# Fused linear attention and long convolution on one core: two stretches of the hand-written schedule put in a new order, with fourteen steps on other engines

## The chip, the cores and the metric

The kernel runs on one NeuronCore of a Trainium2 chip. The core's engines each work through their own list of instructions in order and meet only through semaphores: TensorE (PE, with its weight loads shown apart as PEld), VectorE (DVE), ScalarE (ACT), GpSimd (POOL), and SyncE (SP), which here only starts DMA transfers. The metric is the device time of one execution in microseconds. Three timed executions of the kernel before took 295.18, 297.97 and 299.99 us (median 297.97). The profile is of one more execution, which took 295.91 us.

## The reference

Eight batches go through two layers. The first is linear attention over 8 heads, 576 positions and 64 channels:

```python
def phi(x):
    proj = np.einsum('bhsd,df->bhsf', x, w_phi)            # 64 -> 128 features
    proj = proj - np.max(np.abs(proj), axis=-1, keepdims=True)
    return np.concatenate([np.exp(proj), np.exp(-proj)], axis=-1)
q_p, k_p = phi(q), phi(k)
kv  = np.einsum('bhsf,bhsd->bhfd', k_p, v)
num = np.einsum('bhsf,bhfd->bhsd', q_p, kv)
den = np.einsum('bhsf,bhf->bhs', q_p, np.sum(k_p, axis=2))[..., None] + 1e-06
x   = num / den                       # heads side by side: [8, 576, 512]
```

The second is a gated convolution along the sequence, done by Fourier transform:

```python
proj = x @ w_proj                     # 512 -> 3 * 512: x1, x2, x3
conv = irfft(rfft(x2, axis=1) * rfft(filter_fft, axis=0), n=576, axis=1)
out  = (x1 * conv * x3) @ w_out       # float32, [8, 576, 512]
```

## The kernel before

**The plan.** No scheduler and no pool decides the order. `PLAN` (lines 30 to 197) is a long string of words, and `run` (lines 1039 to 1043) calls one method for each word from left to right. A word is the name of a step and its arguments, with the first PSUM bank behind an `@`: `X1,3,1@5` is step X1 of batch 3, block 1, written to bank 5; a step that needs two banks takes the next one as well. Where a step can run on either of two engines, the word names the engine (`Fe,ACT,2,1@0`). Since each engine is in order, the order of the words of one engine is the order of its instructions; semaphores follow from what is read and written. Four batches or so are in flight at once, so the words of one batch stand between those of others.

```python
        for word in PLAN.split():
            name, _, bank = word.partition("@")
            self.bank = int(bank) if bank else None
            f, *args = name.split(",")
            getattr(self, f)(*[int(a) if a.isdigit() else a for a in args])
```

**The steps of one batch b**, in the order of the data:

- `load` (POOL queue, L595) brings q, k or v in; `trh` (SP queue, L607) transposes a half of q or k into qT or kT.
- `Pk`, `Pkt` (PE, L635, L650) project k. Out of PSUM, `ex,k,p` and `ex,k,m` (ACT, L697) take the two exponentials, and `maxk` (DVE, L715) the maximum. `Qn`, `Qnt` project q for `maxq` alone. `mhi` (ACT), `mlo` (DVE or POOL, L739), `trm` (PE) and `trme` (a copy) bring the maxima of q into a transposed form mT; `Pq`, `Pqt` (PE, L669, L675) project q again with them subtracted, and `ex,q` (ACT) takes the exponentials.
- `em` (ACT, L751) and `vs` (POOL, L757) scale v; `KV` (PE, L772) is the sum over positions, `KVe` its copy; `NE`, `NEt` (PE, L786, L795) give numerator and denominator; `rc` and `xn` (DVE, L800, L805) divide. `xn` is written into one buffer, a quarter v at a time.
- `trx` (SP queue, L824) transposes a quarter of xn into xT, `trxt` (L829) the rest; for the last quarter of batch 6 `ptx` and `ptxe` do it on PE and DVE. `X1` and `X3` (PE, L916) read all four quarters of xT.
- `f1`, `f2` (POOL or DVE, L853, L859) are sums and differences of xn for the Fourier transform; `Ft`, `Fs` (PE, L868, L875) transform, `Fe` (a copy, ACT L297 or DVE L299) writes XF, `X2` (PE, L894) projects, `Y1` (DVE, L904) multiplies by the filter, `m3` (POOL, L908) adds, `I` (PE, L969) transforms back; `Ie` (ACT, L987) copies one bank of it, `Ip` and `Im` (DVE, L990) make cv from that copy and the other bank.
- `X1e` (a copy) puts X1 into x1s, `tm` (DVE, L957) multiplies X3 in, `tmt` (DVE, L961) does so for the rest, `ym` (POOL, L1004) multiplies by cv, `yt` (ACT) moves 64 columns, `O` (PE, L1015) projects, `Oe` (a copy, L297 or L299) takes it out of PSUM, and `st` (mostly the SP queue, L1024) stores half of it.

**Buffers.** Most tiles are in rings of two (`RING`, line 25), the q exponentials and the scaled v in rings of three, the staging tile o and the k exponentials in rings of four; xn, XF, xf, x1s and T0 to T4 are single. PSUM has eight banks, and every PE step waits until the last reader of its bank is done.

Of the kernel before, what the change touches and what calls it, by code (L numbers as in the profile page):

```python
# [82 lines left out]
KV,2,1@2 Pk,3,1@6 X1,1,0@4 KVe,ACT,2,1@2 maxk,3,1@6 NE,2,2@0 rc,2,2@0 xn,2,2@0 load,k,5 X2,1,1@5
NE,2,3@2 X1e,ACT,1,0@4 m3,POOL,1,1 X1,1,1@4 Xl,ACT,1 ex,k,p,3,1@6 X2,1,4@0 Y1,1,1@5 ex,k,m,3,1@6
Pqt,2@6 rc,2,3@2 X1e,ACT,1,1@4 xn,2,3@2 Pk,3,0@2 Y1,1,4@0 Pkt,3@4 X1t,1@1 X3,1,3@0 exqt,p,2@6
m3,POOL,1,0 maxkt,3@4 exqt,m,2@6 maxk,3,0@2 I,1,3@6 exkt,m,3@4 exkt,p,3@4 Ie,1,3@6 Im,1,3@6 Ip,1,3@6
st,SP,0,2,0 f1,POOL,2,0,1 f1,POOL,2,1,1 load,v,3 tm,1,3@0 X1te,ACT,1@1 ex,k,p,3,0@2 X3t,1@4
st,SP,0,2,1 trx,2,0 st,SP,0,1,0 tmt,1@4 I,1,1@5 Ie,1,1@5 Im,1,1@5 X3,1,0@7 Ip,1,1@5 X3,1,1@4 trx,2,1
tm,1,0@7 ex,k,m,3,0@2 trx,2,3 I,1,0@2 Ie,1,0@2 ym,POOL,1,3 Ip,1,0@2 tm,1,1@4 Im,1,0@2 NEt,2@6
rct,2@6 xnt,2,1@6 f1,POOL,2,1,0 ym,POOL,1,1 I,1,2@0 Ie,1,2@0 Qnt,3@4 Pk,3,2@2 ex,k,p,3,2@2 xnt,2,0@6  # L90
Im,1,2@0 maxqt,3@4 trh,q,4,1 Ip,1,2@0 trx,2,2 X1,2,0@0 Qn,3,1@6 ym,POOL,1,0 X1e,ACT,2,0@0
st,SP,0,0,1 ym,POOL,1,2 st,SP,0,1,1 ex,k,m,3,2@2 em,m,3,0 Pk,3,3@4 st,SP,0,3,1 X1,2,2@1
f2,POOL,2,0,1 maxq,3,1@6 mhi,3 X1e,ACT,2,2@1 load,v,4 X1,2,1@0 st,SP,0,3,0 yt,ACT,1 trh,q,4,0
st,SP,0,0,0 maxk,3,3@4 mlo,POOL,3 O,1,2@6 ex,k,m,3,3@4 maxk,3,2@2 Oe,ACT,1,2@6 O,1,3@1 em,m,3,1
Oe,ACT,1,3@1 f2,POOL,2,0,0 ex,k,p,3,3@4 trm,3@2 O,1,0@3 X1e,DVE,2,1@0 Ft,2,0,0@6 Fs,2,1@0
f2,POOL,2,1,0 Oe,ACT,1,0@3 Fs,2,0@6 em,p,3,0 st,SP,1,2,0 trxt,2 f2,POOL,2,1,1 Fe,DVE,2,0@6
Fe,ACT,2,1@0 vs,POOL,p,3,0 O,1,1@4 vs,POOL,m,3,0 trh,k,4,0 X3,2,0@3 Oe,DVE,1,1@4 Ft,2,1,4@0 tm,2,0@3
st,SP,1,0,0 Qnt,4@6 Fs,2,3@4 trme,ACT,3@2 Fs,2,2@0 Pq,3,1@2 Fe,ACT,2,3@4 Fe,ACT,2,2@0 ex,q,p,3,1@2
st,SP,1,1,0 ex,q,m,3,1@2 maxqt,4@6 Qn,4,0@6 Pq,3,0@4 X3,2,1@0 X2,2,3@1 X2,2,2@2 ex,q,p,3,0@4
maxq,4,0@6 KV,3,0@6 st,SP,1,3,1 tm,2,1@0 Y1,2,3@1 ex,q,m,3,0@4 em,p,3,1 Qn,4,2@4 Pq,3,2@0  # L100
KVe,ACT,3,0@6 vs,POOL,m,3,1 Y1,2,2@2 Pk,4,1@2 X2,2,0@6 maxq,4,2@4 NE,3,1@4 maxk,4,1@2 rc,3,1@4
Xl,ACT,2 ex,q,p,3,2@0 load,q,5 vs,POOL,p,3,1 xn,3,1@4 ex,q,m,3,2@0 ex,k,p,4,1@2 st,SP,1,2,1
trh,k,4,1 X2,2,1@7 ex,k,m,4,1@2 KV,3,1@0 m3,POOL,2,1 Y1,2,0@6 Y1,2,1@7 Pq,3,3@4 KVe,ACT,3,1@0
NE,3,0@2 ex,q,p,3,3@4 trx,3,1 NE,3,2@0 ex,q,m,3,3@4 X2,2,4@7 load,k,6 m3,POOL,2,0 X1t,2@6 rc,3,0@2
xn,3,0@2 NE,3,3@4 rc,3,2@0 X1te,ACT,2@6 xn,3,2@0 Y1,2,4@7 rc,3,3@4 xn,3,3@4 Pqt,3@0 trx,3,0
exqt,m,3@0 I,2,1@6 Pk,4,0@4 Ie,2,1@6 trx,3,3 Im,2,1@6 f1,POOL,3,0,0 exqt,p,3@0 ex,k,m,4,0@4 Pkt,4@2
Ip,2,1@6 X3t,2@6 X1,2,3@0 tmt,2@6 maxk,4,0@4 X3,2,2@1 NEt,3@6 exkt,p,4@2 trx,3,2 maxkt,4@2 rct,3@6
X1e,ACT,2,3@0 f1,POOL,3,0,1 O,1,4@0 ex,k,p,4,0@4 exkt,m,4@2 tm,2,2@1 trh,k,5,1 f2,POOL,3,0,0
f1,POOL,3,1,0 I,2,0@4 f1,POOL,3,1,1 Oe,ACT,1,4@0 Pk,4,2@2 xnt,3,1@6 xnt,3,0@6 f2,POOL,3,1,0 Qn,4,3@0
maxq,4,3@0 Ie,2,0@4 em,m,4,0 Im,2,0@4 Ip,2,0@4 st,SP,1,4,1 ym,POOL,2,1 ym,POOL,2,0 st,SP,1,3,0  # L110
trh,k,5,0 st,SP,1,4,0 f2,POOL,3,1,1 I,2,3@6 Ie,2,3@6 Ip,2,3@6 X3,2,3@4 tm,2,3@4 ex,k,p,4,2@2 I,2,2@0
f2,POOL,3,0,1 X1,3,0@5 X3,3,0@4 ex,k,m,4,2@2 X1e,ACT,3,0@5 Im,2,3@6 st,SP,1,1,1 Ie,2,2@0 maxk,4,2@2
Ip,2,2@0 X1,3,1@5 Qn,4,1@2 Im,2,2@0 ym,POOL,2,2 em,p,4,0 ym,POOL,2,3 Ft,3,0,6@0 Fs,3,0@0 Fs,3,1@6
trh,q,5,1 load,v,5 Fe,ACT,3,0@0 st,SP,1,0,1 tm,3,0@4 maxq,4,1@2 X1,3,2@4 Pk,4,3@2 Fe,ACT,3,1@6
maxk,4,3@2 mhi,4 Ft,3,1,6@0 mlo,POOL,4 X1e,ACT,3,1@5 vs,POOL,p,4,0 Fs,3,2@0 Fs,3,3@6 O,2,1@5
Fe,ACT,3,2@0 load,k,7 Fe,ACT,3,3@6 Qn,5,3@0 em,p,4,1 em,m,4,1 vs,POOL,p,4,1 X2,3,2@6 ex,k,p,4,3@2
maxq,5,3@0 X2,3,0@7 trm,4@0 ex,k,m,4,3@2 vs,POOL,m,4,0 X1e,ACT,3,2@4 Oe,ACT,2,1@5 Y1,3,2@6 O,2,2@1
Oe,ACT,2,2@1 Y1,3,0@7 X2,3,1@6 trme,ACT,4@0 vs,POOL,m,4,1 Pq,4,0@4 Qn,5,2@0 Y1,3,1@6 Xl,ACT,3
maxq,5,2@0 Pq,4,1@2 ex,q,m,4,0@4 trh,k,6,0 ex,q,p,4,0@4 ex,q,m,4,1@2 O,2,0@7 Oe,DVE,2,0@7
ex,q,p,4,1@2 X2,3,3@6 Y1,3,3@6 st,SP,2,0,1 KV,4,0@4 Pk,5,0@0 Pq,4,3@6 maxk,5,0@0 O,2,3@2  # L120
KVe,ACT,4,0@4 trxt,3 trh,q,5,0 ex,q,m,4,3@6 m3,POOL,3,1 NE,4,0@4 rc,4,0@4 ex,q,p,4,3@6 X3,3,2@3
st,SP,2,1,0 m3,POOL,3,0 xn,4,0@4 KV,4,1@6 Oe,DVE,2,3@2 load,q,6 ex,k,m,5,0@0 tm,3,2@3 ex,k,p,5,0@0
Pq,4,2@4 NE,4,1@0 rc,4,1@0 KVe,ACT,4,1@6 xn,4,1@0 f1,POOL,4,0,1 ex,q,p,4,2@4 NE,4,3@6 X2,3,4@3
rc,4,3@6 xn,4,3@6 ex,q,m,4,2@4 Y1,3,4@3 X1t,3@0 X1te,ACT,3@0 f1,POOL,4,0,0 NE,4,2@4 X3t,3@6 I,3,1@0
rc,4,2@4 f2,POOL,4,0,0 Pk,5,1@2 Ie,3,1@0 xn,4,2@4 tmt,3@6 trx,4,0 Pkt,5@6 Ip,3,1@0 Pqt,4@4 Im,3,1@0
maxkt,5@6 exqt,p,4@4 X3,3,1@0 exqt,m,4@4 f1,POOL,4,1,0 tm,3,1@0 st,SP,2,1,1 X1,3,3@1 exkt,p,5@6
exkt,m,5@6 maxk,5,1@2 I,3,0@4 Ie,3,0@4 ym,POOL,3,1 X1e,ACT,3,3@1 I,3,2@6 Ie,3,2@6 NEt,4@0 Im,3,0@4
Ip,3,0@4 ex,k,m,5,1@2 Im,3,2@6 rct,4@0 Ip,3,2@6 X3,3,3@5 ym,POOL,3,0 ex,k,p,5,1@2 xnt,4,1@0
f1,POOL,4,1,1 I,3,3@6 Ie,3,3@6 trx,4,3 em,m,5,0 trx,4,1 st,SP,2,2,0 xnt,4,0@0 tm,3,3@5 Pk,5,3@2
em,p,5,0 Qn,5,1@0 Ip,3,3@6 Qnt,5@4 trx,4,2 Im,3,3@6 maxq,5,1@0 X1,4,1@6 X3,4,1@7 maxqt,5@4  # L130
ex,k,m,5,3@2 trh,q,6,0 st,SP,2,3,0 ex,k,p,5,3@2 X1e,ACT,4,1@6 Pk,5,2@0 ex,k,p,5,2@0 f2,POOL,4,0,1
tm,4,1@7 ym,POOL,3,3 ex,k,m,5,2@0 Qn,5,0@4 maxq,5,0@4 maxk,5,2@0 ym,POOL,3,2 X1,4,0@6 vs,POOL,m,5,0
O,3,0@7 Oe,DVE,3,0@7 X1,4,2@4 mhi,5 trh,k,6,1 maxk,5,3@2 f2,POOL,4,1,1 X1e,ACT,4,0@6 X1,4,3@5
Ft,4,0,0@6 X1e,ACT,4,3@5 mlo,POOL,5 f2,POOL,4,1,0 Fs,4,1@0 X1e,ACT,4,2@4 trh,q,6,1 Fs,4,0@6 X3,4,2@5
Fe,ACT,4,1@0 yt,ACT,3 em,p,5,1 Fe,ACT,4,0@6 st,SP,3,0,1 trm,5@4 Ft,4,1,0@2 Fs,4,2@2 Fs,4,3@0
tm,4,2@5 Fe,DVE,4,3@0 st,SP,2,2,1 trme,ACT,5@4 Fe,ACT,4,2@2 Pq,5,1@6 Pq,5,0@4 Pk,6,0@2 maxk,6,0@2
O,3,2@0 Oe,DVE,3,2@0 st,SP,2,3,1 X2,4,1@1 ex,q,p,5,1@6 ex,q,m,5,1@6 trh,k,7,1 st,SP,2,0,0
vs,POOL,p,5,1 X2,4,2@6 vs,POOL,p,5,0 Y1,4,1@1 X2,4,3@7 ex,q,m,5,0@4 em,m,5,1 vs,POOL,m,5,1
ex,q,p,5,0@4 Xl,ACT,4 Y1,4,2@6 KV,5,0@4 KVe,DVE,5,0@4 Pqt,5@0 exqt,m,5@0 X2,4,0@6 Y1,4,3@7 NE,5,0@4
rc,5,0@4 xn,5,0@4 load,q,7 exqt,p,5@0 load,v,6 KV,5,1@0 Y1,4,0@6 ex,k,m,6,0@2 Pq,5,3@4 ex,k,p,6,0@2  # L140
KVe,ACT,5,1@0 ex,q,m,5,3@4 NE,5,1@2 rc,5,1@2 st,SP,3,2,1 xn,5,1@2 X2,4,4@0 Pk,6,2@6 ex,q,p,5,3@4
Y1,4,4@0 st,SP,3,0,0 m3,POOL,4,1 Pq,5,2@2 ex,q,m,5,2@2 ex,q,p,5,2@2 maxk,6,2@6 NE,5,3@4 rc,5,3@4
O,3,1@0 Oe,ACT,3,1@0 O,3,3@1 NE,5,2@2 m3,POOL,4,0 xn,5,3@4 O,3,4@0 Oe,DVE,3,3@1 ex,k,p,6,2@6
ex,k,m,6,2@6 rc,5,2@2 xn,5,2@2 NEt,5@4 rct,5@4 xnt,5,1@4 xnt,5,0@4 I,4,3@2 f1,POOL,5,0,1 X3,4,0@1
Ie,4,3@2 Ip,4,3@2 f1,DVE,5,1,1 f1,POOL,5,0,0 trxt,4 f2,DVE,5,0,0 tm,4,0@1 Oe,ACT,3,4@0 X1t,4@0
I,4,1@4 X1te,ACT,4@0 f1,DVE,5,1,0 Ie,4,1@4 Im,4,3@2 Ft,5,0,0@6 trx,5,3 st,SP,3,3,1 Ip,4,1@4
f2,POOL,5,0,1 X3t,4@2 Fs,5,1@0 trx,5,0 Fe,ACT,5,1@0 tmt,4@2 load,v,7 Fs,5,0@6 Im,4,1@4 f2,POOL,5,1,1
f2,POOL,5,1,0 X3,4,3@3 Fe,ACT,5,0@6 Ft,5,1,0@4 tm,4,3@3 Pk,6,1@6 trx,5,1 Fs,5,3@0 ym,POOL,4,1
# [932 lines left out]
```

## Time and profile before

| | |
|---|---|
| three timed executions | 295.18, 297.97, 299.99 us |
| profiled execution, its span | 295.91 us, 294.0 us |
| granted TensorE clock | 0.996 (mean) |
| PE, PEld busy | 272.7 us (93%), 194.9 us (66%) |
| DVE, ACT, POOL busy | 248.8 (85%), 223.5 (76%), 229.4 (78%) us |

Of the profiled execution's 295.91 us, 1.9 lie outside the span. All times within the trace count from the span's start. Busy times are averages over stages that differ: what a stage is worth is read from its own window, from the chain that ended last, and from what each engine waited for. Starts of PE steps follow each other more closely than their durations, since matmuls overlap in the pipeline.

### The profile page before, as it was taken

The numbers are of one execution on the slowest core, as the hardware profiler recorded it, in microseconds if no ns is written. First come the engines' busy times: TensorE is split into PE (matmuls) and PEld (weight loads), VectorE is DVE, ScalarE is ACT, GpSimd is POOL, SyncE is SP. The second block draws the span as 40 slices with busy tenths as digits, with TensorE's granted clock in tenths as the row PEclk, the third lists the DMA queues.
The fourth block names the chain that finished last, engine by engine and source line by source line (L and its number), as shares of the span: only waits on it lengthen the run. The fifth ranks groups of instructions, "written<-read, shape, count | busy, mean of one in ns | idle before, by whom it ended". The sixth has DMA issues, their size and how long they took to land.

```text
span 294.0 us, 10233 instructions
## 1 busy us (share of the span) xinstructions
PE 272.7 (93%) x4297; PEld 194.9 (66%) x4332; DVE 248.8 (85%) x433; ACT 223.5 (76%) x371; POOL 229.4 (78%) x187
## 2 busy tenths in 40 slices
...
GB/s 138 240 207 163 164 197 168 123 203 181 131 157 199 151 162 195 161 107 187 172 112 138 211 95 108 161 138 180 61 98 50 90 75 28 21 45 56 61 130 188
DMA packets 72191, 40.07 MB, mean 136 GB/s; under 512 B 52496, under 2 KB 66960, under 8 KB 72144
## 3 DMA queue, kind: packets, MB, share of 16 engines
...
q10 hardware_dynamic: 400, 0.66, 0.8%
...
## 4 chain that ended last, share of the span: by engine, by line
PE 63%; DVE 5%; DMA 4%; issue 2%; ACT 2%; POOL 1%; SPq 0%; DVEq 0%; ACTq 0%; POOLq 0%
PE ps L916 15%; PE ps L894 10%; PE ps L1015 8%; PE ps L969 7%; PE ps L772 5%; PE ps L786 4%; PE ps L875 2%; PE ps L925 2%; PE ps L669 2%; PE ps L635 2%; DMA qT<-qn 2%; PE ps L675 2%; DVE mq L715 2%; PE ps L642 2%; DMA xT<-xn 1%
## 5 line engine op out<-in xcount | busy, mean ns | idle before, releaser
L916 PE MATMUL ps<-xT,wproj 128*128 128x256 bf16 x512 | 64.1, 273 | 0.5 <-DMA xT<-xn 0.4
L916 PEld LDWEIGHTS <-wproj 128*128 128x128 bf16 x512 | 48.1, 98 | 9.5 <-issue 0.6
L1004 POOL TENSOR_TENSOR yT<-cv,x1s 128x576 bf16<-128x576 f32 x31 | 39.3, 1278 | 18.5 <-DVE cv L990 16.9
L715 DVE TENSOR_REDUCE mq<-ps 128x8 f32<-128x1024 f32 (+1 forms) x40 | 43.7, 1110 | 4.1 <-PE ps L642 3.6
L715 DVE TENSOR_REDUCE mk<-ps 128x8 f32<-128x1024 f32 (+1 forms) x40 | 43.9, 1111 | 3.8 <-PE ps L635 2.6
L757 POOL TENSOR_TENSOR vm<-vn,vm 128x1152 bf16<-128x1152 bf16 x16 | 34.3, 2152 | 5.9 <-ACT vm L751 5.9
L757 POOL TENSOR_TENSOR vp<-vn,vp 128x1152 bf16<-128x1152 bf16 x16 | 34.4, 2155 | 5.6 <-ACT vp L751 5.5
L853 POOL TENSOR_TENSOR SD<-xn 128x512 bf16<-128x512 bf16 x28 | 32.0, 1153 | 7.0 <-DVE xn L805 5.4
L697 ACT ACTIVATE Eqp<-ps 128x1024 bf16<-128x1024 f32 x32 | 33.1, 1039 | 4.6 <-PE ps L675 4.5
L859 POOL TENSOR_TENSOR xf<-SD 128x512 bf16<-128x512 bf16 x27 | 30.8, 1155 | 6.7 <-DVE SD L853 6.2
L1015 PE MATMUL ps<-wout,yT 128*128 128x512 bf16 x127 | 34.8, 379 | 1.1
L697 ACT ACTIVATE Ekp<-ps 128x1024 bf16<-128x1024 f32 x32 | 33.1, 1034 | 1.9 <-PE ps L635 1.4
L697 ACT ACTIVATE Ekm<-ps 128x1024 bf16<-128x1024 f32 x32 | 33.1, 1033 | 1.3 <-DVE mk L715 0.9
L697 ACT ACTIVATE Eqm<-ps 128x1024 bf16<-128x1024 f32 x32 | 32.8, 1040 | 1.5 <-PE ps L675 1.1
L990 DVE TENSOR_TENSOR cv<-es,ps 128x288 f32<-128x288 f32 x64 | 26.4, 443 | 6.5 <-POOL yT L1004 3.7
L908 POOL TENSOR_TENSOR T<-T,T 128x1024 bf16<-128x1024 bf16 x14 | 29.6, 2127 | 2.7 <-DVE T L904 1.9
L894 PE MATMUL ps<-wproj,XF 128*128 128x512 bf16 x116 | 30.0, 379 | 1.2 <-ACT x1s L297 0.4
L969 PE MATMUL ps<-inv,T 128*128 128x288 bf16 x192 | 28.1, 286 | 0.7 <-DVE mq L715 0.4
L297 ACT COPY o<-ps 128x512 f32<-128x512 f32 x23 | 13.5, 596 | 15.9 <-PE ps L1015 13.7
L957 DVE TENSOR_TENSOR x1s<-ps,x1s 128x512 bf16<-128x512 f32 x32 | 21.8, 684 | 3.5 <-PE ps L916 2.2
L297 ACT CAST XF<-ps 128x576 bf16<-128x576 f32 x28 | 16.9, 647 | 9.2 <-PE ps L875 9.2
L297 ACT CAST x1s<-ps 128x512 bf16<-128x512 f32 (+1 forms) x32 | 16.9, 538 | 8.6 <-PE ps L916 4.2
(183 smaller groups left out, 638.2 us busy)
## 6 DMA issues: line engine op xcount, KB each, us to landing
out_dram<-o SPq DMA_DIRECT2D x67, 128.0 KB, 2.5
...
fl<-in_moe_filter_fft_dram SPq DMA_DIRECT2D x8, 128.0 KB, 6.2
out_dram<-o ACTq DMA_DIRECT2D x5, 128.0 KB, 2.8
...
```

Source lines behind the costliest of these rows:

```text
L297: self.nc.scalar.copy(dst, src)
L697: self.nc.scalar.activation(e, p, AF.Exp, bias=0.0, scale=1.0 if g == "p" else -1.0)
L715: self.nc.vector.tensor_reduce(out=out, in_=src, axis=AX.X, op=ALU.max, apply_absolute_value=True)
L757: self.eng(eng).tensor_tensor(out=t[:, :, :, 0:64], in0=self.at("vn", b)[:, 2 * X:2 * X + 2], in1=t[:, :, :, 64:65].to_broadcast([128, 2, ...
L853: self.eng(eng).tensor_tensor(out=o[:, :, 2 * i:2 * i + 2, :], in0=x[:, :, 0:2, :], in1=x[:, :, 2:4, :], op=ALU.subtract if i else ALU.add)
L859: self.eng(eng).tensor_tensor(out=o[:, :, 2 * i:2 * i + 2, :], in0=x[:, :, 0:4:2, :], in1=x[:, :, 1:4:2, :], op=ALU.subtract if i else ALU ...
L894: self.mm(self.pb(0), l, w[:, kt, 512:1024], start=(kt == 0), stop=(kt == 3))
L908: self.eng(eng).tensor_tensor(out=Y, in0=Y, in1=self.at(f"T{2 * e + 1}", b), op=ALU.add)
L916: self.mm(o[:, d], w[:, kt, f0 + 128 * m:f0 + 128 * m + 128], y[:, 1, ::-1, ::-1] if d else y[:, 0], start=(kt == 0), stop=(kt == 3))
L969: self.mm(self.pb(e, 0, 288), l, inv[:, 2 * e + i if i < 2 else 4 + e, :], start=(i == 0), stop=(i == 2))
L1004: self.eng(eng).tensor_tensor(out=self.at("yT", b)[:, m, 0:SEQ], in0=self.turn_of("cv", (b, m)).rearrange("p x h t -> p (x h t)"), in1=sel ...
L1015: self.mm(self.pb(0), y[:, kt, 128 * c:128 * c + 128], w[:, kt, :], start=(kt == 0), stop=(kt == 3))
```

## The change

Only the plan changes. The number of words stays, and so does what each computes. From `trh,k,3,1` (line 78 of both files) to batch 4's first `Pq`, and again from batch 5's transform to batch 7's, the words stand in another order; PSUM banks are dealt out anew from there to the end. Fourteen steps change engines:

- from ACT to DVE: `X1e,2,2`, `Oe,1,3`, `Fe,2,1`, `Fe,2,2`, `Oe,4,3`, `Oe,5,3`, `Fe,6,2`, `Fe,6,3`
- from DVE to ACT: `X1e,2,1`, `Fe,2,0`, `X1e,5,3`, `trme,6`
- from DVE to POOL: `mlo,6`; from POOL to DVE: `f2,6,1,0`

Of the moved words, those that the prediction speaks of: `tm,1,3` goes ahead of `Im,1,3`; `load,v,5` goes from before batch 4's `vs` to behind `f1,4,1,0`; `yt,1` and `yt,5` go further back in ACT's list; `trxt,5` goes ahead of three of batch 5's `trx`; `trh,q,5,1` goes ahead of four stores of batch 1 that stood in front of it; the four `trx,3` go out in the order 1, 3, 0, 2 in place of 1, 0, 3, 2; `X1,3,1` becomes the first X1 of batch 3; the four `I,2` all use banks 2 and 3 (before: 6, 4, 6 and 0); `Pk,7,1`, `Ft,6,0`, `Fs,6,0`, `Fs,6,1` and `trm,7` go ahead of `X1,6,0`.

```diff
-f2,DVE,1,1,0 em,p,2,1 X1e,DVE,1,3@6 Fs,1,0@0 Fs,1,1@4 Ft,1,1,2@6 Fs,1,2@6 vs,POOL,p,2,1 Fs,1,3@2
-Fe,ACT,1,0@0 trh,k,3,0 trxt,1 Fe,ACT,1,1@4 Fe,DVE,1,2@6 NE,2,1@0 rc,2,1@0 Fe,ACT,1,3@2 X2,1,3@4
...
+trh,k,3,1 X1,1,3@6 ex,q,p,2,0@2 X1e,ACT,1,2@7 st,SP,0,2,1 em,m,2,1 Ft,1,0,4@0 f2,DVE,1,0,0
...
+vs,POOL,p,2,1 Fs,1,3@2 st,SP,0,0,1 Fe,DVE,1,2@6 trh,k,3,0 Fe,ACT,1,1@4 trxt,1 NE,2,1@0 rc,2,1@0
```

**SP's queue at the start of the first stretch.** kT1 is batch 3's transposed k (two halves, `trh,k,3,1` and `trh,k,3,0`), xTt1 is `trxt,1`, o0 to o3 are staging tiles of batch 0's output, xT0 is batch 2's. Before:

```order
L607 DMA_TRANSPOSE kT1_85<-kn1_79 128x9x128 x2
L829 DMA_TRANSPOSE xTt1_136<-xnt1_132 128x2x128
L1024 DMA out_0_dram<-o1_1175 64x512 x2
L824 DMA_TRANSPOSE xT0_133<-xn0_130 128x4x128
L1024 DMA out_0_dram<-o0_1174 64x512
```

Now:

```order
L607 DMA_TRANSPOSE kT1_85<-kn1_79 128x9x128
L1024 DMA out_0_dram<-o1_1175 64x512
L1024 DMA out_0_dram<-o3_1177 64x512
L607 DMA_TRANSPOSE kT1_85<-kn1_79 128x9x128
L829 DMA_TRANSPOSE xTt1_136<-xnt1_132 128x2x128
L1024 DMA out_0_dram<-o2_1176 64x512
```

Two stores now stand between the two halves of batch 3's k.

**DVE's list where batch 2 is transformed back.** L990 makes cv, mk0 holds the maxima of batch 4's k, L961 is `tmt,2`, L957 `tm,2,2`, rt1 and xnt1 are batch 3's rest. Before:

```order
L805 TENSOR_TENSOR xn0_130<-ps_61,r3_127 128x2x4x64
L990 TENSOR_TENSOR cv0_1170<-es0_1168,ps_61 128x9x32 x2
L961 TENSOR_TENSOR x1s0_141<-ps_61,x1s0_141 128x4x64
L715 TENSOR_REDUCE mk0_86<-ps_61 128x2x4
L715 TENSOR_REDUCE mk0_86<-ps_61 128x2x2
L811 RECIPROCAL rt1_129<-ps_61 128x8
L957 TENSOR_TENSOR x1s0_141<-ps_61,x1s0_141 128x2x8x32
```

Now:

```order
L805 TENSOR_TENSOR xn0_130<-ps_61,r3_127 128x2x4x64
L715 TENSOR_REDUCE mk0_86<-ps_61 128x2x2
L715 TENSOR_REDUCE mk0_86<-ps_61 128x2x4
L990 TENSOR_TENSOR cv0_1170<-es0_1168,ps_61 128x9x32 x2
L961 TENSOR_TENSOR x1s0_141<-ps_61,x1s0_141 128x4x64
L957 TENSOR_TENSOR x1s0_141<-ps_61,x1s0_141 128x2x8x32
L811 RECIPROCAL rt1_129<-ps_61 128x8
```

The two reduces go ahead of the two halves of cv, on which the next `I` in the same banks waits.

**ACT's list where batch 6's q begins.** Ekp3 and Ekm3 are exponentials of batch 7's k, mh0 is `mhi,6`, es0 and es1 are `Ie` of batch 5, o0 is `Oe,4,2`, o1 `Oe,4,0`, mT0 `trme,6`, Eqp0 and Eqm0 `ex,q,6,0`. Before:

```order
L697 ACTIVATE Ekp3_97<-ps_61 128x1024
L735 CAST mh0_90<-mq0_88 128x2x18
L697 ACTIVATE Ekm3_111<-ps_61 128x1024
L987 COPY es0_1168<-ps_61 128x288
L297 COPY o0_1174<-ps_61 128x512
L987 COPY es1_1169<-ps_61 128x288
L297 COPY o1_1175<-ps_61 128x512
L987 COPY es0_1168<-ps_61 128x288
L697 ACTIVATE Eqm0_112<-ps_61 128x2x16x32
```

Now:

```order
L697 ACTIVATE Ekm3_111<-ps_61 128x1024
L697 ACTIVATE Ekp3_97<-ps_61 128x1024
L735 CAST mh0_90<-mq0_88 128x2x18
L987 COPY es0_1168<-ps_61 128x288
L987 COPY es1_1169<-ps_61 128x288
L297 COPY o0_1174<-ps_61 128x512
L297 COPY mT0_92<-ps_61 128x128
L697 ACTIVATE Eqp0_98<-ps_61 128x2x16x32
```

`Oe,4,0` and the third `Ie` no longer stand ahead of the first exponentials of batch 6's q, and the copy of mT has come over from DVE.

236 lines of the change are left out of this document (118 added, 118 removed).

## The prediction

> **What bounds the kernel now.** I read the page's busy times first, then windows that I cut by what the change touches: the first stretch (78 to 150, in three parts), what lies between, the second stretch (192 to 282, in four), and the tail.
>
> ```profile
> span 294.0 us, 10233 instructions
> PE 272.7 (93%) x4297; PEld 194.9 (66%) x4332; DVE 248.8 (85%) x433; ACT 223.5 (76%) x371; POOL 229.4 (78%) x187
> core 0: us, PE busy (x) PEld busy (x) DVE busy (x) ACT busy (x) POOL busy (x), PEclk, DMA share, GB/s
> 78.00:105.00 27.00, 26.16 (x402) 19.69 (x405) 24.68 (x43) 18.66 (x30) 20.53 (x16) 1.00 1.12 175
> 105.00:138.00 33.00, 32.71 (x527) 24.13 (x532) 28.86 (x43) 28.40 (x49) 31.52 (x26) 1.00 1.21 152
> 138.00:150.00 12.00, 11.24 (x120) 6.43 (x119) 9.75 (x11) 9.40 (x18) 11.97 (x10) 1.00 1.14 183
> 150.00:192.00 42.00, 41.51 (x785) 30.94 (x791) 35.59 (x57) 36.12 (x57) 38.28 (x28) 1.00 0.81 133
> 192.00:204.00 12.00, 11.95 (x143) 8.80 (x143) 10.08 (x22) 7.84 (x15) 8.15 (x8) 1.00 1.08 181
> 204.00:222.00 18.00, 17.88 (x261) 13.06 (x261) 17.31 (x25) 11.02 (x23) 12.88 (x8) 1.00 0.53 82
> 222.00:241.00 19.00, 17.24 (x315) 12.48 (x314) 16.60 (x28) 18.08 (x29) 14.45 (x14) 1.00 0.36 60
> 241.00:282.00 41.00, 40.49 (x569) 30.26 (x572) 30.54 (x55) 22.25 (x39) 26.43 (x18) 1.00 0.27 52
> ```
>
> In every window but the tail PE is nearly full, at a granted clock of 1.00. Its idle time is what a new order can win, since no matmul is removed: 0.84 + 0.29 + 0.76 = 1.89 us in the first stretch, 0.05 + 0.12 + 1.76 + 0.51 = 2.44 in the second, 4.33 in all. Waits that hide in the overlap of matmuls come on top, but most of it is in two places: 138 to 150, where POOL has 0.03 us left, and 222 to 241, where ACT and DVE are as full as PE. The chain that ended last says what came late there (start, length, what):
>
> ```profile
> 138.22 4.99 DMA qT<-qn
> 231.78 0.61 DVE xn L805
> 233.28 4.04 DMA xT<-xn
> 239.15 1.19 ACT XF L297 x2
> ```
>
> In the first stretch it is `trh,q,5,1`, sent too late. In the second it is DVE's list up to `xn,6,2`, the transpose behind it, and two copies of XF on ACT.
>
> **First stretch, part by part.** Four places where PE, DVE or a queue is met by the new order:
>
> ```profile
> 97.69 0.82 DVE L990 TENSOR_TENSOR cv<-es,ps 128x288 f32<-128x288 f32 x2 [0.36 <-ACT es L987]
> 127.18 0.69 DVE L805 TENSOR_TENSOR xn<-ps,r 128x512 bf16<-128x512 f32 x1
> 128.11 0.82 DVE L990 TENSOR_TENSOR cv<-es,ps 128x288 f32<-128x288 f32 x2 [0.25 <-ACT es L987]
> 129.53 1.82 DVE L715 TENSOR_REDUCE mk<-ps 128x8 f32<-128x1024 f32 x2
> 122.55 8.39 SPq L824 DMA_TRANSPOSE xT<-xn  x4
> DMA to landing us min/median/max: 5.6/6.0/6.5
> 143.26 0.40 PE L642 MATMUL ps<-wphi,qT 64*128 64x128 bf16 x8 [0.66 <-DMA qT<-qn]
> 141.43 0.81 POOL L595 DMA_DIRECT2D vn<-in_v_dram  x1
> ```
>
> *DVE at 97.* DVE stands 0.36 us still before batch 1's first cv, because ACT's copy isn't there. `tm,1,3` now goes ahead and fills the gap. DVE is 24.68 of 27 busy here, so the list behind it comes sooner: −0.3.
>
> *The transpose of q.* Without the four stores in front, `trh,q,5,1` goes out some 4 us sooner, and the 0.66 before `Qn,5,3` goes. What is late next is POOL, 11.97 of 12. Its list loses `load,v,5` (0.81) there, which is just about what is won: −0.7. The load now comes about 20 us later, to a place with gaps; I cost it at nothing (up to +0.8, the same row, if the gaps are gone).
>
> *Batch 2's I in one pair of banks.* `I,2,0` waits for both halves of the cv of `I,2,1`. DVE is done with `xn,3,3` at 127.18 + 0.69 = 127.9; then come two reduces (1.82) and only then cv (0.82): done at 130.5. In the new order PE gets there at about 130.0, since it is full up to here. I take +0.5. Bounds: 0, if DVE is ahead by the 0.3 above and more; +1.8, if the reduces count in full.
>
> *The order of batch 3's transposes.* `trx,3,3` needs that same `xn,3,3` and now goes ahead of two that were ready. Four issues took 8.39 us from 122.55 to 130.94; now three of them come after 127.9, at some 1.3 each (the last three would end at 131.8, 0.9 later). The last landed between 5.6 and 6.5 us after its issue. `X1,3,1` is also wanted 0.7 sooner than the first X1 was, as one I (below: 0.73) no longer precedes it. Bounds: 0, if the landings are as short as the page's median below, and 0.9 + 0.7 = +1.6. I take +0.5, nearer to the short landings, because a transpose and two stores have left this time.
>
> *The copies.* Four steps go from ACT to DVE and two the other way: two more on DVE, 1.4 us (0.69 and 0.76, rows below). Between 105 and 138 DVE has 33 − 28.86 = 4.1 us free and PE no wait for it. Cost nothing; +1.4 if that room lies elsewhere.
>
> *The stores ahead of batch 3's k.* Nothing, or a rival (below). The first stretch comes to −0.3 − 0.7 + 0.5 + 0.5 = 0.0.
>
> **Second stretch.** First what a step costs on either engine (mean ns before the bar's second part), then where DVE stood still ahead of `xn,6,2`, and PE's wait:
>
> ```profile
> L299 DVE COPY o<-ps 128x512 f32<-128x512 f32 x13 | 8.9, 687 | 3.7 <-PE ps L1015 3.1 <-DMA out_dram<-o 0.4
> L299 DVE CAST XF<-ps 128x576 bf16<-128x576 f32 x4 | 3.0, 755 | 3.0 <-PE ps L875 3.0
> L299 DVE COPY mT<-ps 128x128 bf16<-128x128 bf16 x4 | 0.9, 218 | 0.2 <-PE ps L743 0.2
> L739 DVE TENSOR_TENSOR mh<-mq,mh 128x36 bf16<-128x36 f32 x1 | 0.2, 185 | 0.0
> L859 DVE TENSOR_TENSOR xf<-SD 128x512 bf16<-128x512 bf16 x5 | 1.9, 417 | 0.0
> L859 POOL TENSOR_TENSOR xf<-SD 128x512 bf16<-128x512 bf16 x27 | 30.8, 1155 | 6.7 <-DVE SD L853 6.2
> xT<-xn SPq DMA_TRANSPOSE x28, 4.3
> 217.84 0.69 DVE L957 TENSOR_TENSOR x1s<-ps,x1s 128x512 bf16<-128x512 f32 x1 [0.30 <-PE ps L916]
> 223.68 1.23 DVE L715 TENSOR_REDUCE mq<-ps 128x8 f32<-128x1024 f32 x1 [0.38 <-PE ps L642]
> 217.81 1.47 PE ps L969 x12
> 237.37 0.82 PE L916 MATMUL ps<-xT,wproj 128*128 128x256 bf16 x6 [0.45 <-DMA xT<-xn]
> ```
>
> (The chain's row of 1.47 for twelve matmuls gives the 0.73 of one I.)
>
> *DVE up to `xn,6,2`.* It loses `X1e,5,3`, `mlo,6` (0.19) and `trme,6` (0.22) and gains `Oe,4,3`, a copy of the size of `X1e`, which I set equal: −0.4. The two gaps shown (0.30, 0.38) come from PE steps that waited on ACT's exponentials; these now start sooner, as `Oe,4,0` and an `Ie` no longer precede them: I count both, −0.6. `xn,6,2` comes 1.0 sooner, and with it the transpose: −1.0. Bounds: 0, if another engine is late instead, and −1.8, all of PE's idle there.
>
> *PE at `X1,6,0`.* `Pk,7,1`, `Ft,6,0` and both `Fs` now run while the transpose lands, so the 0.45 is covered: −0.4. They need `trm,7`'s bank and DVE's copies in time; if not, 0.
>
> *XF on two engines.* `Fe,6,2` and `Fe,6,3` run on DVE beside the other two on ACT, and `yt,5` leaves ACT: of the 1.19 in the chain I take −0.3, as 0.755 on DVE is dearer and the change adds 0.69 + 1.51 + 0.42 = 2.6 us to DVE here.
>
> *SP's queue.* `trxt,5` waits ahead of three of batch 5's transposes; they land some 3 us later, about when `X1,5,1` wants them: +0.2 (0 to +0.8).
>
> *`f2,6,1,0` on DVE* costs 0.42 for 1.16 on POOL, off the path: 0. POOL stood still around the `f2` that DVE ran before:
>
> ```profile
> 82.39 2.16 POOL L757 TENSOR_TENSOR vp<-vn,vp 128x1152 bf16<-128x1152 bf16 x1 [2.81 <-ACT vp L751]
> ```
>
> so the price with POOL at work isn't in the trace; bound +1.2, POOL's own `f2` in full. The Trainium skill (SBUF — State Buffer, Who interferes with whom) says that a DVE instruction with two SBUF inputs excludes a GpSimd instruction that reads SBUF, and the later one waits. By that rule this edit would cost up to the 1.2, and the sum below would be −0.3; no run so far shows it.
>
> The second stretch comes to −1.0 − 0.4 − 0.3 + 0.2 = −1.5, and so does the whole. The profiled execution would take 295.91 − 1.5 = 294.4. It lies 2.1 under the median of the three timed executions; the mean of all four is 297.3, and 297.3 − 1.5 = **295.8**.
>
> **The rivals.**
>
> *A: DVE becomes the bound.* From 222 to 241 DVE has 2.4 us free and gets 2.6 (above). If those fall ahead of what PE waits for, the −1.5 is given back, and the time is 297.3. For it: 16.60 of 19, and DVE is in the chain there. Against: most of the additions come behind `xn,6,2`.
>
> *B: slower, by batch 3's k.* Rows: the two transposes before (the second alone took until it landed what the second row says), the last copy of batch 0's output, and the step that needs them:
>
> ```profile
> 76.69 6.81 SPq L607 DMA_TRANSPOSE kT<-kn  x2
> DMA to landing us min/median/max: 8.9/8.9/8.9
> 78.79 0.69 DVE L299 COPY o<-ps 128x512 f32<-128x512 f32 x1
> 89.78 0.39 PE L635 MATMUL ps<-wphi,kT 64*128 64x128 bf16 x8
> out_dram<-o SPq DMA_DIRECT2D x67, 128.0 KB, 2.5
> ```
>
> `trh,k,3,0` now waits for the copy (79.48) and a store's issue, and starts at about 80.1; 8.9 later is 89.0, just ahead of `Pk,3,1` at 89.78. From there each us is one of PE's. If the two stores' 2.5 each go before it in the rings, it lands at 94: +4.2 here, −1.5 there, +2.7: 300.0. If they run beside it, nothing.
>
> *C: faster by over 2%.* PE's busy time hides waits inside overlapping matmuls. If 222 to 241 could be as dense in weight loads as 150 to 192 (30.94/42 = 0.74), its 12.48 would need 16.9 us: −2.1 where idle time alone says −1.8; with all other idle (2.6) and the hidden waits of the first stretch in the same measure, about −6: 291.3. The Trainium skill (Perfetto Trace Analysis, Identifying the Most-Contended Engine) says that matmul busy share misjudges the distance to the limit and the weight loads' share is the better measure: by it, 66% leaves more room than 93%. Against it, from the trace: twelve matmuls of one kind in 1.47 leave no gap.
>
> That the change does nothing of what it says is excluded by the lists.
>
> **How the numbers follow.** The forecast has 0.50, A 0.25, B 0.17, C 0.08. Two per cent, 6.0 us, is about what a measurement of this kernel can tell from no change, as three executions lie 4.8 apart. Neither the forecast nor A reaches it; half of C and the forecast's far end do (0.07), and B only with more late transfers (0.05). The range: down, 3.7 of the 4.33 under the fastest execution, 295.18, is 291.5; up, rival B at 300.0. It holds A and most of the forecast.
>
> **What would show it.** Right: the wait on qT at `Qn,5,3` gone; PE's idle from 222 to 241 under 1; `xn,6,2` about 1 us sooner; no wait of PE for XF. Wrong: a wait of L635 on kT near 90 (B); L969 waiting for DVE's cv or L916 for xT between 128 and 136 at over 1 us each; DVE above 18 of 19 up to `X1,6,0` (A); DVE's `xf` well above 0.42 (the lock).

## The result, and the profile after

Over 20 executions of each kernel the changed one takes 293.86 us in the median and the one before 295.89; the ratio is 0.9939, with a 95% interval of 0.9917 to 0.9962, so 1.8 us are won (1.1 to 2.5); the forecast was 1.5. Some executions of several kernels here, the changed one among them, take some us more than the rest of the same kernel; the ratios leave them out, and where a trace below is of such an execution, its time beside that kernel's range shows it.

The profiled execution takes 293.85 us, its span is 292.1. The windows are those of the prediction.

```profile
span 292.1 us, 10270 instructions
PE 274.5 (94%) x4332; PEld 194.5 (67%) x4332; DVE 252.6 (87%) x437; ACT 222.0 (76%) x367; POOL 228.6 (78%) x187
78.00:105.00 27.00, 27.00 (x419) 20.22 (x417) 25.42 (x44) 19.11 (x32) 20.90 (x17) 1.00 1.26 171
105.00:138.00 33.00, 33.00 (x537) 23.92 (x534) 29.99 (x46) 27.98 (x47) 32.41 (x26) 1.00 1.05 156
138.00:150.00 12.00, 12.00 (x189) 7.43 (x189) 10.73 (x10) 10.71 (x20) 11.61 (x9) 1.00 0.89 132
150.00:192.00 42.00, 41.30 (x728) 30.45 (x722) 34.93 (x57) 35.29 (x56) 38.21 (x29) 1.00 1.00 147
192.00:204.00 12.00, 12.00 (x153) 8.65 (x152) 10.35 (x20) 8.07 (x16) 7.71 (x8) 1.00 1.05 175
204.00:222.00 18.00, 17.99 (x262) 12.93 (x260) 17.24 (x24) 11.96 (x23) 12.97 (x8) 1.00 0.48 80
222.00:241.00 19.00, 18.06 (x331) 13.26 (x329) 17.64 (x31) 17.27 (x27) 14.23 (x13) 1.00 0.34 55
241.00:282.00 41.00, 40.82 (x557) 29.85 (x552) 32.93 (x59) 20.06 (x37) 25.76 (x18) 1.00 0.31 64
```

In the first stretch PE has no idle time left; before it had 0.84, 0.29 and 0.76. Between the stretches, where the change hardly touches the order, it has more than before: 0.70 against 0.49. From 222 to 241 it has 0.94 against 1.76. From 78 to 285 the waits of PE that have a name are down to two (us in total, times, longest):

```profile
PE ps L916 <- DMA xT<-xn: 0.7, 1, 0.7
PE ps L786 <- ACT Eqm L697: 0.3, 1, 0.3
```

The waits on qT and on batch 6's xT are gone. The 0.7 is another one: batch 4's `X1,4,1`, which didn't wait before.

**PE's lead.** To add up the terms one needs how far PE is ahead at each point, though its steps stand in another order. I gave each step the usual distance from its start to the next start in the trace of before (an X1 0.87 us, a Pk 0.22), added these up along each plan, and compared the times at which the same amount of work was done. Each trace's own offset at 84, ahead of all changes, is taken off. In us, negative is ahead of the kernel before at that time of its trace:

| kernel | 112 | 140 | 148 | 164 | 172 | 216 | 228 | 236 | 244 | 268 |
|---|---|---|---|---|---|---|---|---|---|---|
| changed | −0.9 | −1.0 | −1.7 | −1.7 | −0.9 | −1.0 | −1.7 | −1.4 | −1.9 | −2.1 |
| run 3 (load of v at its old place) | −1.0 | −1.1 | −1.9 | −1.8 | −1.8 | −2.1 | −2.7 | −2.4 | −2.9 | −2.8 |
| run 5 (first stretch alone, load old) | −1.0 | −1.1 | −1.9 | −1.9 | −1.8 | −1.4 | −1.4 | −1.4 | −1.5 | −1.5 |
| run 2 (second stretch alone) | 0.0 | 0.0 | −0.1 | −0.1 | −0.1 | +0.2 | −0.5 | −0.1 | −0.6 | −0.9 |
| run 6 (qT's word alone) | 0.0 | 0.0 | −0.7 | −0.7 | −0.7 | −0.9 | −0.9 | −0.9 | −1.1 | −1.1 |
| run 7 (`tm,1,3` back, load old) | −0.4 | −0.5 | −1.2 | −1.2 | −1.2 | −1.4 | −2.1 | −1.7 | −2.3 | −2.4 |
| run 9 (`KVe,6,0` on DVE, load old) | −1.0 | −1.1 | −1.9 | −1.8 | −1.8 | −2.1 | −2.3 | −1.7 | −2.3 | −1.9 |
| run 10 (changed, again) | −1.0 | −1.1 | −1.9 | −1.9 | −1.3 | −1.5 | −2.2 | −1.8 | −2.4 | −2.0 |

The leads repeat from trace to trace to about 0.2 as long as no transfer is late. The changed kernel wins 0.9 to 1.0 by 112 and 0.7 at 143, loses 0.8 between 164 and 168, and wins 1.1 from 216 on. Each of these four was put to the test.

### The profile page after: what moved, and what is told of

It is laid out like the page before. It is cut to its first block, busy times and chain, and to the rows that moved or that the text cites. A ratio compares the mean times of both kernels' runs of the same rounds, so it can differ in the third digit from the quotient of the medians.

```text
span 292.1 us, 10270 instructions
## 1 busy us (share of the span) xinstructions
PE 274.5 (94%) x4332; PEld 194.5 (67%) x4332; DVE 252.6 (87%) x437; ACT 222.0 (76%) x367; POOL 228.6 (78%) x187
## 4 chain that ended last, share of the span: by engine, by line
PE 66%; DMA 5%; DVE 3%; ACT 2%; issue 1%; SPq 0%; DVEq 0%; ACTq 0%
PE ps L916 16%; PE ps L894 11%; PE ps L1015 9%; PE ps L969 6%; PE ps L772 5%; PE ps L786 4%; PE ps L875 3%; DMA out_dram<-o 2%; PE ps L925 2%; PE ps L669 2%; DMA xT<-xn 2%; PE ps L635 2%; PE ps L675 2%; PE ps L642 2%; PE ps L868 1%
## 5 line engine op out<-in xcount | busy, mean ns | idle before, releaser
L916 PE MATMUL ps<-xT,wproj 128*128 128x256 bf16 x512 | 64.1, 273 | 0.7 <-DMA xT<-xn 0.7
L916 PEld LDWEIGHTS <-wproj 128*128 128x128 bf16 x512 | 48.1, 98 | 9.6 <-issue 1.0
L1015 PE MATMUL ps<-wout,yT 128*128 128x512 bf16 x144 | 35.7, 379 | 0.1
L859 POOL TENSOR_TENSOR xf<-SD 128x512 bf16<-128x512 bf16 x26 | 29.7, 1155 | 6.5 <-DVE SD L853 6.0
L894 PE MATMUL ps<-wproj,XF 128*128 128x512 bf16 x128 | 31.6, 379 | 0.4 <-ACT x1s L297 0.4
L990 DVE TENSOR_TENSOR cv<-es,ps 128x288 f32<-128x288 f32 x64 | 26.3, 445 | 5.7 <-ACT es L987 4.4
L969 PE MATMUL ps<-inv,T 128*128 128x288 bf16 x192 | 28.1, 286 | 0.7 <-DVE mq L715 0.4
L957 DVE TENSOR_TENSOR x1s<-ps,x1s 128x512 bf16<-128x512 f32 x32 | 21.8, 686 | 3.1 <-PE ps L916 1.8
L805 DVE TENSOR_TENSOR xn<-ps,r 128x512 bf16<-128x512 f32 x32 | 21.9, 690 | 0.9
L297 ACT COPY o<-ps 128x512 f32<-128x512 f32 x20 | 11.8, 600 | 14.3 <-PE ps L1015 14.2
```

Of the source, the lines that this page charges most:

```text
L297: self.nc.scalar.copy(dst, src)
L859: self.eng(eng).tensor_tensor(out=o[:, :, 2 * i:2 * i + 2, :], in0=x[:, :, 0:4:2, :], in1=x[:, :, 1:4:2, :], op=ALU.subtract if i else ALU ...
L894: self.mm(self.pb(0), l, w[:, kt, 512:1024], start=(kt == 0), stop=(kt == 3))
L916: self.mm(o[:, d], w[:, kt, f0 + 128 * m:f0 + 128 * m + 128], y[:, 1, ::-1, ::-1] if d else y[:, 0], start=(kt == 0), stop=(kt == 3))
L969: self.mm(self.pb(e, 0, 288), l, inv[:, 2 * e + i if i < 2 else 4 + e, :], start=(i == 0), stop=(i == 2))
L1015: self.mm(self.pb(0), y[:, kt, 128 * c:128 * c + 128], w[:, kt, :], start=(kt == 0), stop=(kt == 3))
```

## The experiments

All are edits of the plan, and the times are compared with executions of the kernel before on the same chip.

### Runs 1 and 2: each stretch alone

Run 1 has the changed plan up to batch 5's first `Pq` and the old one behind it, run 2 the other way round.

```diff
 # run 1: words 0 to 971 of the changed plan, then words 972 to 1535 of the plan before
 # run 2: words 0 to 971 of the plan before, then words 972 to 1535 of the changed plan
```

> The new order in the first stretch alone (up to batch 5's first Pq), the old one behind it. Theory 1, the reading of the changed kernel's trace by work done on PE: PE is 1.7 us ahead at 160, loses 0.8 at X1,4,1 and is 0.9 to 1.0 ahead from 170 on, so the whole is 0.9 under the kernel before, with the 0.7 wait of PE for xT at X1,4,1 again. Theory 2, the prediction's sum: the first stretch comes to 0.0. Theory 3, the gain of the first stretch is given back, since what waits in the old second stretch is a late engine and not a late PE: 0, with a longer wait of PE between 222 and 241.

> The old order up to batch 5's first Pq, the new one behind it. Theory 1, the reading of the changed kernel's trace: between 216 and 264 PE gains 1.1 us, so the whole is 1.0 to 1.1 under the kernel before. Theory 2, the prediction's sum: 1.5 under it. Theory 3, the second stretch only gains because the first one hands it over earlier: 0.

Run 1 took 295.7 us against 295.8, ratio 0.9993 (0.9967 to 1.0020). Run 2 took 295.64, ratio 1.0007 (0.9978 to 1.0035). Neither by itself shows a gain, though both together are worth 0.9939. The traces say part of why. Where the two plans meet, their banks don't fit: the first `Pq` of batch 5 takes a bank pair that copies of XF still read, and PE waits there, in run 2 and in run 5 alike:

```profile
PE ps L669 <- DVE XF L299: 0.3, 1, 0.3
```
```profile
PE ps L669 <- ACT XF L297: 0.6, 1, 0.6
```

The lead drops by 0.55 in run 2 and by 0.64 in run 5 at this seam, which belongs to neither kernel. Apart from it run 2 wins 1.1 between 216 and 268, just as the changed kernel does. Run 1's profiled execution (299.84; its others go from 294.1 to 302.9) stands still on batch 4's xT, which is what runs 3 and 4 are about. With the seam taken off, the two times would still add up to less than the 1.8 of both, within intervals of 0.8 us to either side; that remainder is not explained.

### Runs 3 and 4: where batch 5's v is loaded

In run 3 the load goes back to its old place on POOL, in run 4 to the middle between the two.

```diff
 # run 3
+load,v,5 vs,POOL,p,4,0
 ...
-f1,POOL,4,1,0 ... load,v,5
+f1,POOL,4,1,0
 # run 4
+vs,POOL,m,4,1 load,v,5
```

> The changed kernel with batch 5's load of v back ahead of batch 4's first vs on POOL (where it stood before). Theory 1, the load slows batch 4's transposes, which landed up to 8.4 us after their issue: the 0.7 wait of PE for xT at X1,4,1 goes, the landings come down to 6.6 at most, and the time is 0.8 under the changed kernel's; POOL's list from 140 on moves back by 0.8, which would take up to 0.4 of that again if KV of batch 4 waits for it. Theory 2, the landing is long because of the transposes' own order and the store and the transposes of q and k beside them: the wait stays, and the time is that of the changed kernel or up to 0.7 above it, if qT at Qn,5,3 is late again.

> The changed kernel with batch 5's load of v behind batch 4's last vs on POOL, some 11 us earlier than in the changed kernel (at about 149.6), where POOL stands still for 0.4 us. Theory 1 (the load slows the transposes beside it): it is in by about 158.2 (8.6 after its issue), before trx,4,1 goes out at 158.5, so the 0.7 wait at X1,4,1 goes and the time is 0.8 under the changed kernel's, but trx,4,0, which goes out at 153.5, lands later by 1 to 2 us; if the first X1 of batch 4 waits for that one, less. Theory 2 (the load isn't the cause): the wait stays, no change.

Run 3 took 292.76 us, ratio 0.9908 (0.9887 to 0.9929), its six executions within 0.8 us. Here are the load in the timeline of the changed kernel, batch 4's first X1 behind it, and the same X1 in that of run 3 (its plan takes one line less, so its line numbers are one lower):

```profile
160.97 0.78 POOL L595 DMA_DIRECT2D vn<-in_v_dram  x1
165.73 0.44 PE L916 MATMUL ps<-xT,wproj 128*128 128x256 bf16 x2
166.84 1.69 PE L916 MATMUL ps<-xT,wproj 128*128 128x256 bf16 x14 [0.67 <-DMA xT<-xn]
```
```profile
165.47 1.92 PE L915 MATMUL ps<-xT,wproj 128*128 128x256 bf16 x16
```

In the one, two matmuls run and fourteen wait (in the row of fourteen the next X1 begins, `X3,4,1`); in the other, sixteen run through. The four transposes of batch 4 landed so long after their issue, before, changed, and in run 3:

```profile
DMA to landing us min/median/max: 4.5/5.6/6.6
```
```profile
DMA to landing us min/median/max: 5.2/6.7/8.4
```
```profile
DMA to landing us min/median/max: 3.8/4.9/6.4
```

PE waits for the last of the four, which landed 6.2 us after its issue in the changed kernel and 4.3 in run 3. It took 6.2 again in run 10, and 8.1 in runs 1 and 12, which have the load at this place too; in the nine traces with the load at its old place it took 3.6 to 5.3. So theory 1 holds as to the place: with the load of 576 KB issued at 160.97, this transpose lands 1.9 us later. PE's lead keeps its 1.8 past 164. Of the 0.8 that POOL was to lose nothing is seen.

How the load does it is shown in part. In runs 1 and 12 its data go first: for 2.5 us (from 166.5 and from 166.0) 517 and 510 KB of the queue of loads move, and 0 and 4 KB of the queue of transposes and stores; the transpose ends behind that. In the changed kernel and in run 10 the load's data begin to move only when the awaited transpose is nearly through. There the time goes earlier, in a near standstill of all transfers from 160.6 to 163.0 (run 10: 160.9 to 163.2), which run 3 has only from 161.9 to 163.0. It begins about where the load is issued, but what makes it longer stays open.

Run 4 is the failure of the pair: 298.21 us in the median, from 293.13 to 300.27, ratio 0.9962 (0.9928 to 0.9996), which rests on four of its twelve executions. Its profiled execution (298.98) has PE waiting 3.4 us for batch 3's rest, xTt, which goes out at 149.25, just as the load does, and lands after 10.6 us (in the changed kernel after 4.0). I take no price from it; it only says that this place is worse still.

### Run 5: the first stretch alone, with the load at its old place

> The new order in the first stretch alone, but with batch 5's load of v where it stood before. Theory 1 (the load's place hides what the first stretch wins; the trace of the third run, by work done on PE, is 1.85 ahead from 144 to 184 and 2.0 at 216): 1.8 under the kernel before, ratio 0.994, with executions close together as in the third run (0.8 apart), and no wait of PE for xT between 150 and 172; the second stretch is then worth what is left to the third run's 0.9908, some 0.9 us. Theory 2 (the two stretches need one another, whatever the load does): the ratio stays at 0.999 as in the first run.

It took 294.99 us, ratio 0.9983 (0.9965 to 1.0001). PE's lead is 1.85 up to 172, as theory 1 has it, and there is no wait for xT; then the seam takes 0.64, and 1.5 are left at 268. The time shows only 0.5. The profiled execution, the longest of its twelve, was 1.7 behind at 80 already, where no word differs from the kernel before. In the other traces that offset is between 0 and 0.6, so part of what the times spread by lies ahead of anything that is studied here, and a total says less than a lead.

### Run 6: the transpose of q alone

```diff
-trh,k,5,1 ... st,SP,1,4,1 st,SP,1,3,0 trh,k,5,0 st,SP,1,4,0 st,SP,1,1,1 ... trh,q,5,1
+trh,k,5,1 trh,q,5,1 ... st,SP,1,4,1 st,SP,1,3,0 trh,k,5,0 st,SP,1,4,0 st,SP,1,1,1
```

> The kernel before with one word moved: the second half of batch 5's q goes out behind the second half of batch 5's k, ahead of four stores of batch 1 and the first half of batch 5's k, about 4 us sooner. The prediction's term: the 0.66 wait of PE before Qn,5,3 goes and POOL, 11.97 of 12 busy, isn't late behind it: 0.7 under the kernel before (0.9976). Rival, the next late thing: what PE wins there it gives back at the next wait, for the first half of batch 5's k, which now lands later, or in the stretch up to 222, which ends with DVE: 0.

It took 294.92 us, ratio 0.9987 (0.9971 to 1.0003); the forecast of 0.9976 lies inside, but so does no change, and the lead has to decide. It jumps from 0.0 to 0.73 at 143 and stays: the rival, that it is given back, falls. What the rival started from did come, for the first half of batch 5's k landed 3 us later than before (147.4 against 144.4), but PE did not wait for it. Here is how long the transpose of q took before and in run 6:

```profile
DMA to landing us min/median/max: 5.0/5.0/5.0
```
```profile
DMA to landing us min/median/max: 3.2/3.2/3.2
```

It is not only issued sooner, it also lands sooner after its issue; run 12 comes back to that.

### Runs 7 and 8: what won 1.0 by 112

Both start from run 3. Run 7 puts `tm,1,3` back behind the cv of `I,1,3` on DVE, run 8 puts `X3,1,1` back ahead of `I,1,0` on PE. In both a moved step's PSUM bank is shared with another step by then, so that a strip of batch 1 is computed from values that were overwritten; in run 8 this also adds a long wait.

```diff
 # run 7
-tm,1,3@3 ... Im,1,3@6 Ip,1,3@6
+Im,1,3@6 Ip,1,3@6 tm,1,3@3
 # run 8
-I,1,0@6 ... X3,1,1@3
+X3,1,1@3 I,1,0@6
```

> The third run's kernel with batch 1's tm,1,3 back behind the two halves of cv of I,1,3 on DVE. The prediction took 0.3 for this edit: PE, which is 1.0 ahead of the kernel before from 108 on, is then 0.7 ahead, with a gap of DVE of 0.4 to 0.5 before Im,1,3. Theory 2, the other gap (0.70 before Ip,1,0) is what PE gained from: PE stays 1.0 ahead. Theory 3, DVE's list is the bound from 97 to 108 and every gap counts in full: 0.5 ahead.

> The third run's kernel with X3,1,1 back ahead of I,1,0 on PE, so that I,1,0 and with it DVE's cv come 1.0 later. DVE's second gap of the kernel before (0.70, before Ip,1,0) isn't in the prediction. If that gap is the larger part of what the first stretch won at 104 to 108, PE is 0.3 to 0.5 ahead of the kernel before from 108 on, and the gap is there again at 0.5 or more. If tm,1,3 is the whole of it, PE stays 1.0 ahead.

Run 7's lead is 0.4 at 112 where run 3 has 1.0: the edit costs 0.64. DVE's timeline in the kernel before (the row that the prediction didn't quote), in the changed kernel (three rows), and in run 7:

```profile
101.47 0.46 DVE L990 TENSOR_TENSOR cv<-es,ps 128x288 f32<-128x288 f32 x1 [0.70 <-ACT es L987]
```
```profile
97.36 0.68 DVE L957 TENSOR_TENSOR x1s<-ps,x1s 128x512 bf16<-128x512 f32 x1
98.03 0.82 DVE L990 TENSOR_TENSOR cv<-es,ps 128x288 f32<-128x288 f32 x2
99.34 0.82 DVE L990 TENSOR_TENSOR cv<-es,ps 128x288 f32<-128x288 f32 x2 [0.16 <-ACT es L987]
```
```profile
98.34 0.82 DVE L990 TENSOR_TENSOR cv<-es,ps 128x288 f32<-128x288 f32 x2 [0.59 <-ACT es L987]
```

With `tm,1,3` back, the gap is back at 0.59, and PE is 0.64 later: theory 3, DVE's list is the bound here and a gap counts in full. The kernel before had 0.36 + 0.70 = 1.06 of them, run 7 0.59, the changed one 0.16; PE is ahead by 0, 0.4, and 0.9 to 1.0. Run 8 lost 1.4 (its lead at 112 is +0.4), but with a gap of 1.63 ahead of a cv that waits for `X3,1,1`, a wait of the edit's own. It can't tell what the second gap alone is worth; that was not settled.

### Run 9: what holds PE from 222 to 241 now

Run 3 with `KVe,6,0` on DVE in place of ACT, five words further back.

```diff
-KVe,ACT,6,0@6
+KVe,DVE,6,0@6 Im,5,1@4
```

> The third run's kernel with one copy of batch 6 (KVe,6,0, 0.59 on ACT at 224.7 in the changed kernel) on DVE, to tell which engine holds PE from 222 to 241 now. In the changed kernel ACT works from 224.7 to 231.6 without a gap, and PE waits 0.31 before NE,6,2 for its last exponential of batch 6. Theory 1, ACT is the bound: that wait goes and PE is 0.3 to 0.5 further ahead at 232, and keeps it: 0.3 to 0.5 under the third run. Theory 2, DVE's list up to xn,6,2 is the bound, as the prediction had it: xn,6,2 comes some 0.5 later, PE gets a wait for xT at X1,6,0 of 0.3 to 0.5, and at 240 nothing is won or up to 0.5 lost. Theory 3, both: 0.3 won at 232, as much lost at X1,6,0, and 0 at 240.

It took 293.77 us, ratio 0.9931 (0.9903 to 0.9958), 0.5 above run 3's plan on the same chip (run 11), though the intervals overlap; and its lead is 0.4 behind run 3's at 228 and 0.65 from 232 to 260. PE's waits from 222 to 241, in the changed kernel and in run 9:

```profile
PE ps L786 <- ACT Eqm L697: 0.3, 1, 0.3
```
```profile
PE ps L682 <- DVE mq L715: 0.7, 1, 0.7
PE ps L786 <- ACT Eqm L697: 0.4, 1, 0.4
PE ps L786 <- DVE xn L805: 0.2, 1, 0.2
```

The copy takes 0.7 on DVE and costs PE 0.65: DVE has no room here, as theory 2 has it, but PE meets its list at another place, not at `X1,6,0` through the transpose, but already at `Pqt,6` (L682), which waits for the maxima of batch 7's q to free its bank. What half a microsecond less on ACT would be worth by itself this run can't show.

### Runs 10 to 12: side by side on one chip

Run 10 is the changed kernel, run 11 run 3's plan, run 12 the kernel before with the load of v alone at its new place.

```diff
 # run 12, on the kernel before
-load,v,5 (behind ym,POOL,2,3)
+f1,POOL,4,1,0 load,v,5
```

> The changed kernel once more, for a comparison with the next two on the same chip. Theory 1 (the load of v beside batch 4's transposes costs it up to 0.8 in most executions and more in a few): ratio 0.993 to 0.996, with executions spread over 3 us or more. Theory 2 (the spread is that of any kernel here): ratio 0.993, spread like the next run's.

> The third run's kernel once more, with twice the executions. Theory 1: ratio 0.990 to 0.992, some 0.9 under the changed kernel, executions within 1.5 us of each other. Theory 2: the same time and spread as the changed kernel.

> The kernel before with batch 5's load of v alone moved to its new place on POOL. Theory 1 (beside batch 4's transposes the load makes them land late): a wait of PE for xT between 160 and 175 of 0.5 us or more, which the kernel before doesn't have, and the time 0.5 to 1.0 above the kernel before, in some executions 3 to 5 above it. Theory 2, the prediction's price: nothing, 0; and the wait for qT at Qn,5,3 may shrink, as the load no longer goes out beside that transpose.

The changed kernel took 294.39 us, ratio 0.9962 (0.9932 to 0.9991); run 11 took 293.23, ratio 0.9929 (0.9901 to 0.9957), a little above the 0.990 to 0.992 of theory 1. Both times, in run 3 and in run 11, the old place of the load comes out about 1 us under the new one, but in both the intervals overlap, and the old place has six executions only. Run 10's executions go from 293.06 to 302.63, run 11's from 292.74 to 295.08. Run 10's trace has the same wait again:

```profile
166.91 1.69 PE L916 MATMUL ps<-xT,wproj 128*128 128x256 bf16 x14 [0.52 <-DMA xT<-xn]
```

Run 11's trace, of its longest execution (295.08), has no wait there, but another one, ahead of it: PE waits for `Y1` of DVE (L904), whose list had stood still until a store had freed a staging tile.

```profile
149.83 0.69 DVE L299 COPY o<-ps 128x512 f32<-128x512 f32 x1 [1.29 <-DMA out_dram<-o]
151.70 0.28 PE L669 MATMUL ps<-qT,wphi 64*128 64x256 bf16 x2 [1.19 <-DVE T L904]
```

That store went out at 143.20, beside the load (140.47, 9.1 us), and landed after 6.5 us; in run 3's trace stores there took up to 7.2, and nobody waited for them; in the changed kernel, without the load there, they took 2.5 to 4.3. So the old place isn't free either: it cost PE nothing in run 3's trace and 1.2 us in run 11's.

Run 12 took 296.48 us, ratio 1.0017 (0.9994 to 1.0041): 0.8 above in the median, as theory 1 has it, but the interval takes in no change. In its trace the last of batch 4's transposes lands after 8.1 us in place of 4.5, and PE stands 2.8 us still for it (the row is shown in the last section). The load no longer goes out at 141.4, and batch 5's q, whose transpose is issued at 138.1 as in the kernel before, lands after 3.3 us in place of 5.0:

```profile
DMA to landing us min/median/max: 3.3/3.3/3.3
```

The wait at `Qn,5,3` is gone here too, without the transpose going out a moment sooner (PE is 0.7 ahead at 148). So moving the load took one wait away and brought another. The second is borne out by the other traces (runs 1, 3 and 10). The first rests on this trace alone, though run 2, with the load at its old place, has the 5.0 again, and it is not shown that the load's data slowed q. In the kernel before, the load goes out only at 141.43, and its data begin to move at about 143.6, when q was in (143.2); in run 12 q was in at 141.41. What the kernel before does show just ahead of q's landing is a near standstill of all transfers, from about 142.4 to 143.0; run 12 has one too, to 142.8, with q already in. Why q was not in by then in the kernel before stays open.

## Why the prediction was right, and where it was not

The profiled execution was to take 294.4 and took 293.85; the sum was −1.5 and the lead came to −2.1. The 295.8 stood on a mean of four executions, 297.3, where twenty have a median of 295.89: most of the 1.9 by which it is above the result is the base.

| term | forecast | lead measured |
|---|---|---|
| DVE at 97 | −0.3 | −0.9 to −1.0 |
| transpose of q | −0.7 | −0.7 |
| batch 2's I in one pair of banks | +0.5 | 0 |
| order of batch 3's transposes | +0.5 | 0 |
| load of v, copies, stores | 0 | +0.8, 0, 0 |
| **first stretch** | **0.0** | **−0.9** |
| DVE up to `xn,6,2` | −1.0 | −0.4 at 236 |
| PE at `X1,6,0` | −0.4 | −0.5 |
| XF, `trxt,5`, `f2,6,1,0` | −0.3, +0.2, 0 | none seen |
| **second stretch** | **−1.5** | **−1.1** |

That the sum is near is luck: misses of both signs cancel.

*DVE at 97, mis-sized.* The step looked at one gap, 0.36, and costed it as a part of DVE's slack, though its own windows have 0.84 + 0.29 = 1.13 of PE's idle time from 78 to 138. The next gap on the same list, 0.70, is four instructions on and went as well. Run 7 shows for the first that it counts in full here; for the second that was not settled (run 8).

*Batch 2's I and batch 3's transposes.* Both took the middle of a range whose lower end was the case: "0, if DVE is ahead by the 0.3 above and more". As the two gaps had gone, `xn,3,3` ran at 126.34, 0.8 sooner, and neither L969 nor L916 waits between 126 and 138 in the changed kernel. The two terms hung on the first one, and should have been worked out with it.

*The load of v: a step that failed.* "To a place with gaps; I cost it at nothing (up to +0.8, the same row, if the gaps are gone)." The price came, but not as POOL's time. The step asked where the instruction finds room on its engine and not what it does to the transfers in flight where it goes out: the transpose that PE waits for lands 1.9 us later (changed kernel against run 3). The Trainium skill (DMA: Bandwidth & Descriptors, Issuing engines are not separate DMA queues) says that transfers issued from different engines run on the same 16 DMA engines and interleave. In runs 1 and 12 the load and the transposes do meet there, but they hardly interleave: for 2.5 us nearly all that moves is the load's. The prediction gave rival B just such a mechanism, two stores ahead of a transpose, and did not see the load.

*The transpose of q* came as forecast: sent sooner, the wait is gone (run 6). The prediction did not see that the wait also goes when the load alone is moved (run 12); by what is open.

*DVE up to `xn,6,2`.* The step `xn,6,2` moved as forecast; before and now:

```profile
232.53 0.69 DVE L805 TENSOR_TENSOR xn<-ps,r 128x512 bf16<-128x512 f32 x1
```
```profile
231.30 0.69 DVE L805 TENSOR_TENSOR xn<-ps,r 128x512 bf16<-128x512 f32 x1
```

That is 1.23 sooner, but 1.0 of it PE had brought along from the first stretch; only 0.2 was won here. PE itself was 0.7 further ahead at 228 and 0.4 at 236. Counting both gaps of DVE as gain left out how full the stretch is: DVE is busy for 17.64 of 19, and run 9 shows that 0.7 more on it is 0.65 less for PE. ACT, with 17.27 of 19 and no gap from 224.7 to 231.6, may be a second bound; no run tests it. Rival A named DVE as the bound, but not here: its sign, above 18 of 19, did not come.

*PE at `X1,6,0`.* The cover holds: the two X1 run through from 236.51, without a wait.

```profile
236.51 1.91 PE L916 MATMUL ps<-xT,wproj 128*128 128x256 bf16 x16
```

*Rival B* did not come, and not by much. `trh,k,3,0` started at 80.05, as worked out, and landed 9.8 us later, at 89.9; the step that needs it ran at 89.93 without a wait:

```profile
80.05 3.25 SPq L607 DMA_TRANSPOSE kT<-kn  x1
DMA to landing us min/median/max: 8.4/9.1/9.8
```
```profile
89.93 0.40 PE L635 MATMUL ps<-wphi,kT 64*128 64x128 bf16 x8
```

*`f2,6,1,0` on DVE* took its 0.41, but POOL stood still beside it; in none of the fourteen traces does POOL work beside a DVE step that reads two tiles in SBUF. The Trainium skill (SBUF — State Buffer, Who interferes with whom) says that such a DVE step and a POOL step that reads SBUF exclude each other. Whether they do is shown by no run here.

```profile
237.96 0.41 DVE L859 TENSOR_TENSOR xf<-SD 128x512 bf16<-128x512 bf16 x1
```
```profile
239.52 2.15 POOL L757 TENSOR_TENSOR vm<-vn,vm 128x1152 bf16<-128x1152 bf16 x1 [3.05 <-ACT vm L751]
```

*Rival C* did not come: the idle time of PE is enough for what was won. From 78 to 150 it lost 1.89 of idle time and was 1.7 ahead at 148; from 222 to 241 it lost 0.82, and the lead grew by 0.9 from 216 to 244. Nothing here shows that waits were hidden in the overlap.
